# An FFT convolution on one NeuronCore: a second stage of 32 interleaved blocks with a shuffle, or of 16 wide blocks on rows paired +n and -n

## The chip, the cores and the metric

The kernel runs on one core of a Trainium2 chip. The core has a matrix engine (TensorE, PE in the profile; its weight loads are listed as PEld), three engines for elementwise work (VectorE or DVE, ScalarE or ACT, GpSimd or POOL), and SyncE (SP), which here does nothing but issue DMAs. POOL issues DMAs too. Each engine takes its own instructions in order and waits on semaphores for the others. The metric is the device time of one execution in microseconds (us), and a comparison of two kernels goes by the medians of their runs.

## The reference

Two computations are chained: a gated attention with squared ReLU in place of a softmax, and a gate with a long circular convolution, done as a Fourier transform over the S = 3136 rows.

```python
# u, v: [8, 3136, 256]   z: [8, 3136, 64]
scores = (1.0 / S) * np.matmul(z, z.transpose(0, 2, 1))
attn = np.maximum(scores, 0.0) ** 2
x = u * np.matmul(attn, v)                      # attention's output
proj = x @ w_proj                               # [.., 768]
x1, x2, x3 = proj[..., :256], proj[..., 256:512], proj[..., 512:]
X2 = np.fft.rfft(x2, n=S, axis=1)
H = np.fft.rfft(filter_fft, n=S, axis=0)[None]
x2_conv = np.fft.irfft(X2 * H, n=S, axis=1)
return (x1 * x2_conv * x3) @ w_out
```

## The kernel before

**Rows and chunks.** A row n is split as n = n1 * 49 + n2 with n1 < 64 and n2 < 49. A tile of 128 rows holds two values of n2, 64 rows for each, so that a batch has 25 tiles (NT), the last one half full. The 25 tiles of a batch form seven chunks of 512, 384, 512, 384, 512, 384 and 448 query columns (`CHUNKS`). In the kernel before, tile t holds n2 = t and n2 = 25 + t.

**Attention.** For each chunk, pairs of tiles are scored (`score_mm`, L1299: two 64-row matmuls), ACT takes the ReLU (L1474), ACT or DVE squares (L1481, L1483), and the squares are multiplied with v into two PSUM banks (`weigh`, L1329). A part of the squares is transposed by DMA on SP's queue and used again for another chunk (`mirror`, L1414). `xe` (L1527, DVE) multiplies the sum with u^T.

**Projection.** `add_proj` makes the gate x1 * x3 (`ev3`, L865, DVE) and x2 (L893), and `dft1` (L724) applies the first stage of the transform, a [128, 128] table T1 that does both 64-point transforms of a tile. Its result goes to DRAM (D1).

**Second stage.** `add_spectrum` reads D1 back in eight pieces `qq` of four blocks each. A block is 49 complex numbers as 98 interleaved rows and 256 channels. For each piece: one DMA load (L754), four matmuls of 98x98 tables S2 by 256 columns in two groups (L943), two evictions to `xh`, then on DVE a `stream_shuffle` (L964) that swaps real and imaginary rows, two products with H (L967) and a difference (L970), four matmuls with TZ (L1001), two evictions, and a DMA store to D2 (L1031). The last batch has no shuffle: it forms two products (`mul2`, L974) and runs eight matmuls a piece (L1008) against TZ and a copy of TZ with rows swapped. Its pieces also use buffers of other pools, and its loads may run four ahead (`l_p` has four buffers).

**End.** `add_end` loads D2 by groups of four tiles (L765), applies T4 (L1063), multiplies by the gate (L1070, DVE, one instruction for each stretch of a chunk that the group covers), multiplies by w_out (L1101), evicts and stores (L1128).

**Start.** POOL first issues the loads of v and u for batch 0, and behind them its iota instructions (L447 on), from which DVE and ACT build the tables T1, then S2 in eight steps of 392 columns (L588 to L596, L643, L644) and a ninth for block 0. Once, under batch 0, the filter goes through the same stages and gives H (L792 to L794, L807, L356, L360).

**Order.** The order of the instructions of every engine is written when the kernel is built, by the class `Plan`: it simulates the five engines with the costs that each task names, a task becomes ready from the planned ends of the ones before it, and SP's transfers get a planned landing from `moves`, `late`, `DMA_GO` and `DMA_DONE`. PE takes from three kinds of queue: scores (S), the weighing (W) and the fillers (FA the projection, FB the second stage and the end, FZ the ends of batch 6 that are held back for the last batch). At run time the order is fixed, so whatever is late holds up all that is behind it on its engine.

## Time and profile before

| | |
|---|---|
| median of 3 runs | 1052.53 us |
| lowest and highest | 1052.33, 1054.18 us |
| span of the profiled execution (first to last instruction) | 1056.2 us |
| busy in the span | PE 1002.7, ACT 930.4, DVE 841.3, POOL 175.9 us |
| DMA | 325263 packets, 168.35 MB, 159 GB/s; SP's queue 59.8% and POOL's queue 20.9% of 16 engines |

The profiled execution has a span of 1056.2 us, which is 3.7 us above the median of the runs and 2.0 us above the slowest of them. Durations in the profile are from that one execution. Its page lists for each group of instructions the line, the engine, the operation, the tiles and shapes, the count, the busy time, the mean duration of one, and the idle time of the engine just before the group with what ended it. The timeline lists the instructions in order: start, length, engine, line. A row with "x4" merges four of them. SPq is SP issuing a DMA. The table by stretches lists for each engine the busy time in a stretch with the number of instructions behind it, then the granted clock, the DMA share and GB/s. A matmul's listed duration contains the time until its result is out, in which the next one already runs.

### The profile page before, as it was taken

Reading aid. Unit: us, or ns where it says so; the run is one execution under the profiler, and the core shown is the slowest. Engines: PE = TensorE matmul, PEld = TensorE weight load, DVE = VectorE, ACT = ScalarE, POOL = GpSimd, SP = SyncE. Lnnn points to the kernel's source line nnn. Section 1 sums busy time; section 2 is a strip of 40 time slices with the busy share of each in tenths; the row PEclk is TensorE's granted clock in tenths of the full one; section 3 lists DMA queues with packets and bytes.
Section 4 is the critical chain, followed back from the end, with each engine's and each line's share of the span. In section 5 each row is a group of like instructions: output and inputs, shape, how many; then the busy total and the mean of one; then the engine's idle time right before and its main releaser. Section 6 shows DMA issues by size and latency. Waiting matters only on the chain.

```text
span 1056.2 us, 18580 instructions
## 1 busy us (share of the span) xinstructions
PE 1002.7 (95%) x6335; PEld 511.0 (48%) x6335; DVE 841.3 (80%) x1449; ACT 930.4 (88%) x1326; POOL 175.9 (17%) x355
## 2 busy tenths in 40 slices
PE   5899999999999999999999999999999999999984
PEld 2443444445444544454455444545455444554573
DVE  7976678986889778997789958888788887889673
ACT  7897799997999989997999989989998899889772
POOL 3031301221022120212021310121112120001000
PEclk9999999999999999999999999999999999999997
DMA  9489836889698787898799767997789968786486
GB/s 180 74 165 162 153 76 148 151 158 178 163 162 164 136 177 168 189 154 126 169 204 180 135 139 147 181 202 130 148 163 198 179 129 158 158 187 123 115 247 202
DMA packets 325263, 168.35 MB, mean 159 GB/s; under 512 B 232766, under 2 KB 295230, under 8 KB 325168
## 3 DMA queue, kind: packets, MB, share of 16 engines
q1 hardware_dynamic: 301824, 136.19, 59.8%
q0 software_dynamic: 23344, 30.97, 20.9%
q8 instruction: 50, 0.82, 0.3%
q14 instruction: 45, 0.37, 0.1%
HBM read 90.26 MB, written 53.05 MB: 136 GB/s over the span
## 4 chain that ended last, share of the span: by engine, by line
PE 72%; DVE 9%; DMA 8%; ACT 6%; issue 3%; SPq 1%; POOL 1%; DVEq 0%; ACTq 0%; POOLq 0%
PE ps_o_t L1329 37%; PE ps_s_t L1299 11%; DMA M_t<-A_t 5%; PE ps_m_t L893 3%; PE ps_m_t L859 3%; PE ps_m_t L1101 3%; PE ps_m_t L847 3%; ACT R_t L1474 3%; PE ps_m_t L724 2%; PE ps_m_t L1001 2%; PE ps_m_t L1063 2%; DVE xT_t L1527 2%; PE ps_m_t L943 2%; DVE xh L967 1%; DMA specf<-s_t 1%
## 5 line engine op out<-in xcount | busy, mean ns | idle before, releaser
L1474 ACT ACTIVATE R_t<-ps_s_t 128x1024 f32<-128x1024 f32 (+2 forms) x552 | 488.5, 922 | 34.5 <-PE ps_s_t L1299 26.2
L1329 PE MATMUL ps_o_t<-A_t,v_t 128*128 128x512 bf16 (+2 forms) x2064 | 475.1, 355 | 1.9 <-DVE A_t L1483 1.5
L1329 PEld LDWEIGHTS <-v_t 128*128 128x128 bf16 x2688 | 253.9, 98 | 215.9 <-issue 42.2
L1483 DVE TENSOR_TENSOR A_t<-R_t 128x1024 bf16<-128x1024 f32 (+3 forms) x276 | 298.9, 1090 | 32.2 <-ACT R_t L1474 21.3
L1481 ACT ACTIVATE A_t<-R_t 128x768 bf16<-128x768 f32 (+3 forms) x276 | 257.1, 949 | 10.4 <-DMA M_t<-A_t 7.3
L1299 PE MATMUL ps_s_t<-zT_t 64*128 64x512 bf16 (+2 forms) x1088 | 155.1, 357 | 4.5 <-ACT R_t L1474 4.3
L392 POOL COPY tick<-xT_t 1x1 bf16<-1x1 bf16 x54 | 26.6, 492 | 778.7 <-DVE xT_t L1527 778.7
L1527 DVE SCALAR_TENSOR_TENSOR xT_t<-ps_o_t,uT_t 128x384 bf16<-128x384 f32 (+2 forms) x128 | 69.9, 557 | 26.2 <-PE ps_o_t L1329 16.6
L354 ACT ACTIVATE x_t<-ps_m_t 128x512 bf16<-128x512 f32 (+3 forms) x139 | 73.7, 549 | 17.0 <-PE ps_m_t L847 14.0
L1070 DVE TENSOR_TENSOR yT_t<-ps_m_t,gate_t 128x128 bf16<-128x128 f32 (+4 forms) x166 | 63.1, 425 | 27.3 <-PE ps_m_t L1063 27.1
L1299 PEld LDWEIGHTS <-zT_t 64*128 64x128 bf16 x1088 | 33.1, 94 | 103.2 <-issue 102.3
L865 DVE TENSOR_TENSOR gate_t<-ps_m_t,x_t 128x512 bf16<-128x512 f32 (+2 forms) x110 | 65.6, 618 | 20.0 <-PE ps_m_t L859 16.8
L1329 PE MATMUL ps_o_t<-M_t,v_t 128*128 128x384 bf16 (+2 forms) x336 | 77.8, 345 | 3.3 <-DMA M_t<-A_t 3.3
L358 DVE CAST x_t<-ps_m_t 128x512 bf16<-128x512 f32 (+3 forms) x90 | 54.6, 621 | 22.4 <-PE ps_m_t L893 13.4
L967 DVE TENSOR_TENSOR xh<-xh,H 98x1024 bf16<-98x1024 bf16 x112 | 72.3, 684 | 0.0
L387 POOL DMA_DIRECT2D un_t<-in_u_dram x112 | 59.7, 551 | 6.9 <-issue 4.6
L847 PE MATMUL ps_m_t<-xT_t,wp 128*128 128x512 bf16 (+2 forms) x224 | 57.5, 353 | 2.5 <-DVE xT_t L1527 1.4
L893 PE MATMUL ps_m_t<-wp,xT_t 128*128 128x256 bf16 x392 | 58.2, 273 | 1.5 <-DVE gate_t L865 1.4
L859 PE MATMUL ps_m_t<-xT_t,wp 128*128 128x512 bf16 (+2 forms) x220 | 55.5, 355 | 0.4 <-DVE gate_t L865 0.2
L354 ACT ACTIVATE xh<-ps_m_t 98x512 bf16<-98x512 f32 x86 | 50.5, 614 | 3.7 <-PE ps_m_t L943 2.5
L1329 PE MATMUL ps_o_t<-M2e_t,v_t 128*128 128x512 bf16 (+1 forms) x192 | 51.7, 370 | 1.1 <-DVE xT_t L1527 1.1
L358 DVE CAST s_t<-ps_m_t 128x512 bf16<-128x512 f32 (+2 forms) x66 | 41.4, 630 | 12.6 <-PE ps_m_t L724 10.9
(168 smaller groups left out, 1026.2 us busy)
## 6 DMA issues: line engine op xcount, KB each, us to landing
out_dram<-ost_t SPq DMA_DIRECT2D x82, 256.0 KB
spec_in_t<-spec SPq DMA_DIRECT2D x64, 196.0 KB
spec<-gs_t SPq DMA_DIRECT2D x60, 196.0 KB
spec<-s_t SPq DMA_DIRECT2D x80, 128.0 KB
v_t<-in_v_dram POOLq DMA_DIRECT2D x80, 128.0 KB, 4.1
spec_in_t<-spec SPq DMA_DIRECT2D x39, 256.0 KB
un_t<-in_u_dram POOLq DMA_DIRECT2D x56, 128.0 KB, 4.9
un_t<-in_u_dram POOLq DMA_DIRECT2D x56, 96.0 KB, 4.5
```

Source lines behind the costliest of these rows:

```text
L354: nc.scalar.activation(out_, in_, AF.Copy)
L358: nc.vector.tensor_copy(out_, in_)
L847: nc.tensor.matmul(box["p"][:, :cw], wp16[:, k, ds(nb * P, P)], xt["t"][:, k, :cw], start=(k == 0), stop=(k == 1),)
L859: nc.tensor.matmul(box["p3"][:, :cw], wp16[:, k, ds((4 + nb) * P, P)], xt["t"][:, k, :cw], start=(k == 0), stop=(k == 1),)
L893: nc.tensor.matmul(box["p"][:rows, ds(k_ * D, D)], xt["t"][:, k, ds((i + k_) * P, rows)], wp16[:, k, ds(D, D)], start=(k == 0), stop=(k == 1),
L967: nc.vector.tensor_tensor(xb["z"][:KR, i], xb["z"][:KR, i], H[:KR, qq, i], ALU.mult)
L1299: nc.tensor.matmul(ps[:m, i, :cw], zt[h, ds(t * P, m)], zt[h, ds(C0[c], cw)], start=True, stop=True)
L1329: nc.tensor.matmul(o, row(v16[b], t)[:, ds(dh * P, P)], x, start=(k == 0 and i == 0), stop=(last and i == len(pair) - 1),)
L1474: nc.scalar.activation(box["R"][:rows, 0:n, :cw], live[un][:rows, 0:n, :cw], AF.Relu)
L1481: nc.scalar.activation(a, r, AF.Square)
L1483: nc.vector.tensor_tensor(a, r, r, ALU.mult)
L1527: nc.vector.scalar_tensor_tensor(x, f, inv_s2, ut, ALU.mult, ALU.mult)
```

## The change

The tiles are filled in another order and the second stage is cut in another way. Nothing in what is computed changes.

- **Pairing.** n2 is counted around its middle, so that a tile holds rows n2 and the rows that mirror them (+n and -n). The loads of z, u and v are cut by chunk (`runs`), since the first half of a tile runs backwards through a chunk. `xe` and `ev3` become two instructions each, one for each half, and the first one writes its tiles in reverse order. `add_end` works by chunk: the gate is one instruction for each half of the channels, and T4's matmul writes two stretches of 64 columns.
- **First stage.** T1 gives 32 real and 32 imaginary lines of the pair's sums and differences, so that real and imaginary parts stand side by side in the columns.
- **Second stage.** 16 blocks j (NJ) of 2 x 50 rows. A block is one matmul of a 128x128 real table by 512 columns, 256 real and 256 imaginary (`forward`, `inverse`); block 0 takes four of 256. The product with H has two multiplications with H repeated over the two halves, and two instructions of half the size for the difference and the sum; no shuffle. D1 is read in four loads of four blocks, each of two DMAs of 50 partitions with 4 KB each, and D2 is written likewise. The last batch takes the same way with eight loads and stores of two blocks, two DMAs each; the swapped table and `mul2` are gone.
- **Tables.** S2 and TZ have 19 tables of 128x128 in place of 32 of 98x98. S2 needs two steps of 392 columns and one of 50. H takes 15 matmuls of 512 columns and 4 of 256, and 16 evictions, in place of 64 and 32; its expanded tables (L792 to L794) are gone.
- **Buffers.** `l_p` has two buffers of twice the size, and the loads of the end get their own pool `c_p` with two; `gs_p` doubles. Two memsets on POOL clear the unused rows.

The diff, cut to its core:

```diff
-NQ = 32
-KR = 2 * N2
+NJ = 16
+KB = 50
...
-    gs_p = Pool("gs", 2, [P, 4, D], BF16)
-    l_p = Pool("spec_in", 4, [P, 4, D], BF16)
+    gs_p = Pool("gs", 2, [P, 8, D], BF16)
+    l_p = Ring("spec_in", 2, [P, 8, D], BF16)
+    c_p = Pool("conv_in", 2, [P, 4, D], BF16)
...
+    def runs(lo, hi):
+        got = []
+        for c in range(NC):
+            a, b = max(lo, T0[c]), min(hi, T0[c + 1])
+            if a < b:
+                got.append((0, a, b, NT - T0[c + 1] + a - T0[c]))
+        if lo < min(hi, NT - 1):
+            got.append((1, lo, min(hi, NT - 1), NT + lo))
+        return got
+
+    def halves(c):
+        n = len(tiles[c])
+        return (0, n), (1, n if CHUNKS[c] % P == 0 else n - 1)
+
+    def by_half(x, h, n):
+        return x.rearrange("p (t i) -> p t i", i=P)[:, 0:n, ds(h * N1, N1)]
...
+        for j, lo, hi, n2 in runs(t0, t1):
+            for c in range(home[lo], home[hi - 1] + 1):
+                a, b = max(lo, T0[c]), min(hi, T0[c + 1])
+                nc.gpsimd.dma_start(
+                    out=t[ds(j * N1, N1), ds(v_at(a), (b - a) * D)],
+                    in_=r[:, n2 + a - lo : n2 + b - lo, :].rearrange("p t d -> p (t d)"),
+                )
...
-    load_rows(v16[0], v[0], 0, 8)
+    load_rows(v16[0], v[0], 0, 7)
     u_nat = {}
     cast_u(0, 0)
-    load_rows(v16[0], v[0], 8, NT)
+    load_rows(v16[0], v[0], 7, NT)
+    k1v, k2v, k0v = kcol[:, 0:N1], kcol[:, N1 : N1 + 8 * N2], kcol[:, 456:512]
+    nc.gpsimd.iota(k1v, pattern=[[N2, N1 // 2], [0, 2]], base=0, channel_multiplier=0)
...
-    for q0 in range(0, NQ, 4):
+    for j0 in (0, 8):
...
+            for r in range(2):
+                nc.sync.dma_start(
+                    out=box["t"][ds(r * N1, KB), 0 : 2 * nj, :], in_=by_block(src, r)[:, ds(2 * j0, 2 * nj), :]
+                )
+
+        t = on("SP", go, 0.9, [pads, *deps, *((d, ISSUED) for d in loads[-1:])], [l_p.slots], moves=0.6 * nj, late=late)
...
+    def two_tables(ps, w, x, order):
+        for c, pair in enumerate(order):
+            for k, i in enumerate(pair):
+                nc.tensor.matmul(
+                    ps[:, ds(c * D, D)], w[:, i, :], x[:, ds(k * D, D)], start=(k == 0), stop=(k == 1)
+                )
+
+    def forward(ps, x, j):
+        if j:
+            nc.tensor.matmul(ps[:, :], S2[:, 3 + j, :], x, start=True, stop=True)
+        else:
+            two_tables(ps, S2, x, ((3, 0), (1, 2)))
...
-                    nc.vector.tensor_tensor(
-                        gates[b, c, nb][:, :cw], box["p3"][:, :cw], box["x"][:, :cw], ALU.mult
-                    )
+                    for h, w in halves(c):
+                        g, p, x = (by_half(y, h, w) for y in (gates[b, c, nb], box["p3"], box["x"]))
+                        nc.vector.tensor_tensor(g[:, ::-1] if h == 0 else g, p, x, ALU.mult)
...
+            def mul(i, g=g, xb=xb):
+                x = xb["x"][:].rearrange("p i (j c) d -> p i j c d", c=2)
+                h = H[:, ds(2 * g, 2), i].unsqueeze(2).to_broadcast([P, 2, 2, D])
+                nc.vector.tensor_tensor(x[:, 1 - i], x[:, 0], h, ALU.mult)
+
+            def sums(xb=xb):
+                x = xb["x"][:].rearrange("p i (j c) d -> p i c j d", c=2)
+                nc.vector.tensor_tensor(x[:, 1, 0], x[:, 1, 0], x[:, 0, 1], ALU.subtract)
+                nc.vector.tensor_tensor(x[:, 1, 1], x[:, 1, 1], x[:, 0, 0], ALU.add)
...
+                    for k in range(nt):
+                        lo, hi = (nt - 1 - k) * P, k * P + N1
+                        x = cb["t"][:, k, ds(dh * P, P)]
+                        o = box["p"][:, 0:512]
+                        if hi >= w:
+                            nc.tensor.matmul(o[:, ds(lo, N1)], x, T4[:, 0:N1], start=True, stop=True)
+                            continue
+                        o = bass.AP(o.tensor, o.offset + min(lo, hi), [o.ap[0], [abs(hi - lo), 2], [1, N1]])
+                        nc.tensor.matmul(o, x, T4[:, ds(N1 if lo > hi else 0, P)], start=True, stop=True)
```

## The prediction

> **What bounds the kernel now.** I read the page first, then the table by stretches, the groups by form, and the timeline of start and tail. The stretches from 160 to 1000 us, summed, show an idle PE for 840 - 826.4 = 13.6 us in all; PE sets the pace there, and what DVE and ACT save can give back little of it. The columns are length, then busy time (instructions) of PE, PEld, DVE, ACT, POOL, then clock, DMA share, GB/s.
>
> ```profile
> 0.00:40.00 40.00, 26.42 (x137) 10.51 (x138) 32.40 (x88) 31.99 (x48) 10.56 (x29) 1.00 0.66 121
> 80.00:120.00 40.00, 34.96 (x194) 15.61 (x192) 23.65 (x41) 29.88 (x38) 7.03 (x15) 0.96 1.04 164
> 640.00:680.00 40.00, 40.00 (x282) 20.62 (x280) 33.91 (x57) 38.03 (x53) 5.55 (x12) 1.00 0.89 174
> 1000.00:1040.00 40.00, 28.96 (x234) 22.95 (x233) 25.80 (x55) 24.20 (x47) 0.00 (x0) 0.85 0.81 242
> ```
>
> So the change must be priced in PE time in the middle, and in whatever is late at both ends. The timeline shows what a matmul costs in a row of them, and the start:
>
> ```profile
> 1014.59 0.27 PE L1008 MATMUL ps_o_t<-xh,TZ 98*98 98x256 bf16 x1
> 1014.70 0.27 PE L1008 MATMUL ps_o_t<-xh,zT_t 98*98 98x256 bf16 x1
> ...
> 21.02 2.76 PE L1329 MATMUL ps_o_t<-A_t,v_t 128*128 128x512 bf16 x12
> ...
> 1.51 1.34 POOL L399 DMA_DIRECT2D v_t<-in_v_dram  x2
> ...
> 6.17 0.36 POOL L447 IOTA yT_t<- 128x128 int32 x1
> 6.56 0.47 DVE L612 TENSOR_SCALAR spec_in_t<-yT_t,percol 128x64 f32<-128x64 int32 x2 [2.87 <-POOL yT_t L447]
> 8.18 0.31 ACT L596 ACTIVATE T<-spec_in_t 128x128 bf16<-128x128 f32 x1 [3.45 <-DVE spec_in_t L593]
> 8.39 0.58 ACT L354 ACTIVATE zT_t<-ps_m_t 128x512 bf16<-128x512 bf16 x1
> 9.11 1.04 PE L1299 MATMUL ps_s_t<-zT_t 64*128 64x512 bf16 x4
> ```
>
> A 256-column matmul lasts 0.27 us but the next starts after 0.11; twelve of 512 columns take 2.76, of which 0.38 is the last one's length, so (2.76 - 0.38) / 11 = 0.216 each. And the first scores hang on POOL's iota: POOL's loads, then the iota, DVE, ACT's sine, the copy of z behind it in ACT's queue, the scores. The groups that the change removes or replaces:
>
> ```profile
> L967 DVE TENSOR_TENSOR xh<-xh,H 98x1024 bf16<-98x1024 bf16 x112 | 72.3, 684 | 0.0
> L943 PE MATMUL ps_m_t<-spec_in_t,S 98*98 98x256 bf16 x244 | 43.9, 275 | 0.3
> L964 DVE STREAM_SHUFFLE xh<-xh 128x512 f32<-128x512 f32 x56 | 39.8, 729 | 0.4 <-issue 0.4
> L970 DVE TENSOR_TENSOR xh<-xh 98x1024 bf16<-98x1024 bf16 x56 | 38.7, 692 | 1.7
> L724 PE MATMUL ps_m_t<-x_t,T 128*128 128x512 bf16 x79 | 29.7, 382 | 0.4 <-ACT x_t L354 0.2
> L1195 DVE COPY zd_t<-zn_t 128x1024 bf16<-128x1024 bf16 x21 | 8.8, 419 | 0.2 <-DMA zn_t<-in_z_dram 0.2
> ```
>
> **The change, part by part.**
>
> *PE, per spectrum.* Forward and inverse are 64 matmuls x 0.109 = 7.0 us now and 2 x (15 x 0.216 + 4 x 0.109) = 7.35 after: +0.35, over seven batches +2.5 us. The busy column agrees: single 512-column matmuls show 29.7 / 79 = 0.376 against 2 x 43.9 / 244 = 0.36 for the pair that one replaces. Half as many instructions buy PE nothing.
>
> *DVE, per spectrum.* Gone: 8 shuffles x 0.729 = 5.8 and 8 differences x 0.692 = 5.5. New: 16 half-size instructions. In the rows a DVE instruction has about 0.15 us that doesn't shrink (512 columns from PSUM 0.687, 256 0.416), so each is (0.692 + 0.15) / 2 = 0.42, in all 6.7. The two products stay at 0.684 if H, repeated, is read at full rate; L1195, which repeats its input the same way, takes 0.419 for 1024. Halving `xe` and `ev3` adds 0.15 us for each extra instruction, 12 + 14 = 26 of them: +3.9. The end's gates go from 24 pieces to 14 a batch: -1.5. Sum -2.2 us a batch on an engine that isn't the bound, hidden by PE; at most 13.6 us of PE's idle time could answer to it. `xe` frees PSUM for PE, so some of its 0.15 shows. ACT's evictions stay 16 + 16. DMAs on SP per batch are the same number within two (loads 8 and 8, stores 8 and 8, outputs 13 and 14). POOL issues about 4 more loads of z and 1 of v per batch, 0.55 us each, on an engine busy 17%; the same hides its memsets and the filter's loads, now partly in pieces of 1 KB. The end's loads get two buffers where they shared four, behind W work as before. Late loads (below) can add. Together for the seven spectra: +1 (-6 to +8), nearest to PE's row.
>
> *Start.* Batch 0's v goes out in 4 + 11 POOL DMAs instead of 2 + 4. Nine more at 0.55 (mean of L399) to 0.67 (1.34 / 2) put the iota 5 to 6 us later, and T1 takes four small DVE instructions where two stood, less two memsets: first scores +5.5. DVE, ACT and PE all wait in order behind it, so nothing covers it. z's ten SP DMAs for six come 3 us later at most and are landed by then. Against this, six of eight table steps go from DVE and ACT: 2 x 0.382 + 0.365 + 0.365 + 0.562 + 2 x 0.15 = 2.36 us on DVE and 0.53 on ACT each, 17 us in all. Between 10 and 40 us DVE is busy 27.9 and ACT 28.1 of 30 and PE 24.7, so there they are the bound. With the work shared out, half of it, 8.7 us, is the most it can give, and PE's own idle time of 5.3 is nearer. I take 4. Net +1.5 (-3 to +5).
>
> *H and the tables.* Matmuls for H 64 x 0.109 = 7.0 become 3.7, the transposes lose 0.4; the 16 evictions and the expanded tables (8 x 0.92 on DVE) that go had little to hold up, since DVE and ACT are 59% and 75% busy from 80 to 120 us, where PE's waits are for DMAs that stay. -4 (-8 to -1).
>
> *Tail.* The last batch's second stage runs from the first load at 1007 us to the last store at 1030.3. Its DVE chain goes from 2 x 0.685 to 2 x 0.684 + 2 x 0.42 = 2.2 us a piece, +6.7 over eight; DVE is busy 11.8 of 12 us from 1012 to 1024. PE falls from 96 x 0.109 to 7.35, at a clock of 0.72 in the last 6 us. The loads: four could be out before, two now, each of two DMAs.
>
> ```profile
> 1007.50 1.82 SPq L754 DMA_DIRECT2D spec_in_t<-spec  x3
> 1013.28 3.15 SPq L754 DMA_DIRECT2D spec_in_t<-spec  x4
> 1019.43 0.38 PE L943 MATMUL ps_m_t<-spec_in_t,S 98*98 98x256 bf16 x2
> ```
>
> Already here the fifth piece starts at 1019.43, 6 us after its load was issued. Two at a time, at 3.4 us a landing (the chain's row for the first) plus about 1.5 to issue and compute, make four rounds of 5: last forward at about 1011 + 15 = 1026, then 4.4 us of DVE, inverse, eviction and store: 1033 to 1036 against 1030.3, less what PE saves. The end behind it is 25 tiles as before. +4 (0 to +7).
>
> **Sum.** 1.5 - 4 + 1 + 4 = +2.5. The profiled span of 1056.2 is 3.7 above the median of the runs, 1052.5; I put the differences on the median: 1055.0 us. A change within 0.2%, 2.1 us, I count as none: about what a measurement of this kernel can tell.
>
> **Rivals.**
>
> *Faster: the first 160 us belong to DVE and ACT.* In the start they do, and the work taken from them there is 17 + 7.4 + 16 x 0.63 = 34 us. If they set the pace up to H as well, half, 17 us, comes off, in place of the 8 I count for recovery and H together: 1055.0 - 9 = 1046. It decides once more than 10.5 us are recovered. PE's idle time speaks for it (20.8 us in 160, 8.3 in the first 10), DVE and ACT at 59% and 75% before H against.
>
> *Slower: the blocks land late in all batches.* A load is 392 KB instead of 196, through 50 partitions at a time, and the plan gives it 1.2 + 2.4 + 0.8 + 1.0 = 5.4 us after its issue. If the landing grows with the bytes from 3.4 to 6.8, each is 1.4 late; 28 of them, if PE stood for each, 39 us. PE stood only 2.1 us for such loads at L943 before, the W work ahead of them covers most, and I take a quarter: 1065. It decides when landings pass the planned ones by more than the next PE group. The Trainium skill, "DMA: Bandwidth & Descriptors", section "Why a DMA increments its semaphore by 16 and not by 1", says that a DMA uses the largest number of engines up to 16 that divides the slowest dimension: 14 for 98 rows, but 10 for 50. By that rule each engine carries 40 KB instead of 14, and this rival gains; the views, means over 16 engines, don't show it.
>
> *Slower: no full rate for H repeated.* At the rate of the f32 squares (1.219 for 1024) 16 products cost +0.535 and 16 half instructions +0.27 each, 12.9 us a batch; DVE would then be as busy as ACT, and I put 15 us: 1070. L1195 speaks against it.
>
> **How the numbers follow.** The forecast, parts that nearly cancel, 0.50: its range is 1047 to 1063, of which slower 0.28, within 0.2% 0.17, faster 0.05. Faster rival 0.30 (0.28 faster, 0.02 same), late blocks 0.15, no full rate 0.05. In all: faster 0.33, same 0.19, slower 0.48. The range to the other cases, leaving out a tenth on either side: 1043 to 1066.
>
> **What would show it.** Start: first L1299-type scores near 14.6 us instead of 9.11, with DVE waiting for the iota. Recovery: the first `xe` no later than 37 us (35.4 now). PE: 512-column matmuls of the second stage 0.216 apart, and an idle sum from 160 to 1000 us near 13.6; well above, the late blocks are right. DVE: products near 0.68, sums near 0.42. Tail: last D2 store 3 to 6 us further behind the last weighing. I am wrong if the start isn't delayed, or if PE's waits in the middle change by more than 6 us.

## The result and the profile after

The changed kernel takes 1069.2 us (median of four runs, 1065.5 to 1071.4) where the one before, run beside it, takes 1053.4 (1052.3 to 1056.1). The ratio is 1.0146, with a 95% interval of 1.0116 to 1.0177: slower, as was held likeliest in sign, but by 16 us and not by 2.5, and 3 us past the end of the range.

The profiled execution has a span of 1069.5 us against 1056.2 before, 13.3 more. Split at two points that both traces have, the first `xe` of batch 1 and the first of the very last chunk, it is 2.1 us ahead of the kernel before at the first point, loses 10.9 between the two, and 4.5 in the tail behind the second: -2.1 + 10.9 + 4.5 = 13.3. The medians lie 15.9 apart, so the two profiled executions show a little less than the whole. The forecast had -2.5, +1 and +4. The miss is the middle.

The table by stretches of the changed kernel, with the columns as before (length, busy time and instructions of PE, PEld, DVE, ACT and POOL, then the clock, DMA share and GB/s):

```profile
0.00:40.00 40.00, 17.01 (x91) 6.84 (x92) 22.64 (x59) 21.30 (x34) 17.79 (x37) 1.00 0.68 117
80.00:120.00 40.00, 39.72 (x235) 18.00 (x232) 28.59 (x48) 36.00 (x48) 15.36 (x32) 1.00 1.12 175
640.00:680.00 40.00, 39.78 (x259) 19.42 (x257) 33.50 (x57) 39.66 (x54) 4.38 (x10) 1.00 0.76 169
1000.00:1040.00 40.00, 29.21 (x158) 13.56 (x155) 32.13 (x61) 23.89 (x43) 0.00 (x0) 0.76 0.45 133
```

The first 40 us lost 9.4 us of PE (26.42 before). From 80 to 120 PE is full where it idled 5 us before: the lighter H and tables pay the start back there. The stretch from 640 on looks as before; the middle's loss sits in a few places and has to be looked for. In the last row PE's clock is 0.76 against 0.85. Summed over the 21 stretches of 40 us from 160 to 1000, PE idles 16.5 us against 13.6, which is 2.9 more and far less than the 10.9 lost. Where the rest hides is the first thing to learn here. A matmul at half clock counts as busy, and so does work that the changed kernel does between the two points and the kernel before did elsewhere; both are measured in the account of the prediction below.

The groups that replace those shown of the kernel before:

```profile
L969 DVE TENSOR_TENSOR xh<-xh,H 128x1024 bf16<-128x1024 bf16 x120 | 81.4, 683 | 5.6 <-ACT xh L357 4.7
L793 PE MATMUL ps_m_t<-spec_in,S 128*128 128x512 bf16 x123 | 45.8, 384 | 3.7 <-ACT R_t L1456 1.7 <-DVE gs_t L361 1.0 <-ACT H L359 0.4
L973 DVE TENSOR_TENSOR xh<-xh 128x512 bf16<-128x512 bf16 x60 | 25.3, 422 | 1.7
L974 DVE TENSOR_TENSOR xh<-xh 128x512 bf16<-128x512 bf16 x60 | 25.0, 416 | 0.0
```

The products with H repeated keep their 0.683 us and the sums take 0.42: both as priced, and the rival of a lost rate is out. Nor do the forward matmuls wait for their loads. So the middle lost its time neither to the rate of DVE nor, directly, to late blocks.

The start, in the timeline of the changed kernel:

```profile
7.75 0.52 POOL L416 DMA_DIRECT2D v_t<-in_v_dram  x1 [0.92 <-DMA v_t<-in_v_dram]
...
10.30 0.52 POOL L416 DMA_DIRECT2D v_t<-in_v_dram  x1 [0.66 <-DMA un_t<-in_u_dram]
...
13.38 0.32 POOL L457 IOTA yT_t<- 128x64 int32 x1
13.73 0.85 DVE L630 TENSOR_SCALAR gs_t<-yT_t,percol 128x32 f32<-128x32 int32 x4 [10.24 <-POOL yT_t L457]
16.71 0.31 ACT L616 ACTIVATE T<-gs_t 128x128 bf16<-128x128 f32 x1 [12.42 <-DVE gs_t L612]
18.96 1.03 PE L1281 MATMUL ps_s_t<-zT_t 64*128 64x512 bf16 x4 [0.58 <-ACT zT_t L357]
```

The iota comes at 13.38 instead of 6.17, and the first scores at 18.96 instead of 9.11: 9.85 us, where 5.5 were forecast. From its eleventh DMA on, POOL waits before four of seven for an earlier one to land (0.92, 0.66, 0.59 and 0.23, in all 2.4 us), which the count of issues left out. Behind the iota, the second conversion of z (L361, 0.95 us at 16.59) now stands on DVE behind the steps of the pattern, where ACT had made the first two from 4.01 on in the kernel before, so z's own path to the scores waits for the pattern too.

The largest step of the middle is 6.2 us beside the kernel before, between the fifth and sixth chunk of batch 1. In the timeline of the changed kernel there:

```profile
240.31 0.96 DVE L1465 TENSOR_TENSOR A_t<-R_t 128x768 bf16<-128x768 f32 x1 [3.02 <-DMA M2e_t<-A_t]
...
241.36 0.92 ACT L1456 ACTIVATE R_t<-ps_s_t 128x896 f32<-128x896 f32 x1 [3.27 <-DVE A_t L1465]
241.92 0.38 PE L731 MATMUL ps_m_t<-x_t,T 128*128 128x512 bf16 x1 [2.99 <-DVE x_t L361]
```

DVE's next square stands 3.02 us for a transposing DMA that still reads the buffer it needs; ACT, the copies behind the square, and PE stand with it. What SP's queue did just before, in the kernel before and in the changed one:

```profile
228.19 1.23 SPq L1202 DMA_TRANSPOSE zT_t<-zd_t  x1
...
230.58 1.21 SPq L1158 DMA_TRANSPOSE uT_t<-un_t  x1
231.84 2.33 SPq L1414 DMA_TRANSPOSE M2e_t<-A_t  x1
```

```profile
228.82 0.82 SPq L1016 DMA_DIRECT2D spec<-gs_t  x2
229.74 3.07 SPq L1188 DMA_TRANSPOSE zT_t<-zd_t  x1
232.91 1.23 SPq L1144 DMA_TRANSPOSE uT_t<-un_t  x1
234.19 2.58 SPq L1396 DMA_TRANSPOSE M2e_t<-A_t  x2
```

In the changed kernel the transpose of z, right behind two stores of second-stage blocks, holds SP for 3.07 us instead of 1.23, and the mirrored tile's transposes leave some 2.3 us later. And the clock after the wait, in stretches of one microsecond of the same trace:

```profile
239.00:240.00 1.00, 0.00 (x0) 0.00 (x0) 0.00 (x0) 0.00 (x0) 0.00 (x0) 1.00 1.24 157
...
242.00:243.00 1.00, 1.00 (x5) 0.51 (x5) 1.00 (x2) 0.88 (x2) 0.00 (x0) 0.72 0.42 127
243.00:244.00 1.00, 1.00 (x5) 0.43 (x3) 0.92 (x2) 0.22 (x1) 0.00 (x0) 0.50 0.14 44
244.00:245.00 1.00, 1.00 (x6) 0.20 (x6) 0.51 (x1) 0.38 (x1) 0.00 (x0) 0.50 0.30 90
245.00:246.00 1.00, 1.00 (x9) 0.27 (x8) 0.00 (x0) 0.45 (x1) 0.00 (x0) 0.57 0.00 0
```

After its 2.99 us of rest PE gets half clock for 3.4 us: 0.28 + 0.50 + 0.50 + 0.43 = 1.7 us more, in which it shows as busy. The wait and the clock explain 4.7 of the step's 6.2 us.

### The profile page after: what moved, and what is told of

It reads as the page before. It is cut to its first block, busy times and chain, and to the rows that moved or that the text cites. A ratio compares the mean times of both kernels' runs of the same rounds, so it can differ in the third digit from the quotient of the medians.

```text
span 1069.5 us, 17972 instructions
## 1 busy us (share of the span) xinstructions
PE 998.4 (93%) x6029; PEld 468.0 (44%) x6029; DVE 827.9 (77%) x1492; ACT 914.6 (86%) x1282; POOL 189.9 (18%) x405
## 4 chain that ended last, share of the span: by engine, by line
PE 51%; DVE 7%; DMA 3%; ACT 3%; issue 2%; SPq 1%; DVEq 0%; ACTq 0%
PE ps_o_t L1311 26%; PE ps_s_t L1281 7%; PE ps_m_t L1086 3%; PE ps_m_t L897 2%; PE ps_m_t L866 2%; PE ps_m_t L854 2%; DVE A_t L1465 2%; PE ps_m_t L1055 2%; DVE xh L969 2%; DMA M2e_t<-A_t 2%; PE ps_m_t L799 1%; PE ps_m_t L731 1%; DVE xT_t L1505 1%; PE ps_m_t L793 1%; ACT R_t L1456 1%
## 5 line engine op out<-in xcount | busy, mean ns | idle before, releaser
L1465 DVE TENSOR_TENSOR A_t<-R_t 128x768 bf16<-128x768 f32 (+4 forms) x286 | 305.1, 1073 | 55.7 <-ACT R_t L1456 37.4
L1463 ACT ACTIVATE A_t<-R_t 128x1024 bf16<-128x1024 f32 (+4 forms) x266 | 252.8, 956 | 11.3 <-DMA M2e_t<-A_t 3.3
L406 POOL COPY tick<-xT_t 1x1 bf16<-1x1 bf16 x54 | 10.8, 200 | 760.4 <-DVE xT_t L1505 760.4
L874 DVE TENSOR_TENSOR gate_t<-ps_m_t,x_t 128x256 bf16<-128x256 f32 (+1 forms) x222 | 72.7, 382 | 39.4 <-PE ps_m_t L866 32.0
L1505 DVE SCALAR_TENSOR_TENSOR xT_t<-ps_o_t,uT_t 128x256 bf16<-128x256 f32 (+1 forms) x224 | 76.2, 381 | 26.2 <-PE ps_o_t L1311 14.9
L969 DVE TENSOR_TENSOR xh<-xh,H 128x1024 bf16<-128x1024 bf16 x120 | 81.4, 683 | 5.6 <-ACT xh L357 4.7
L357 ACT ACTIVATE x_t<-ps_m_t 128x512 bf16<-128x512 f32 (+3 forms) x116 | 62.3, 562 | 20.3 <-PE ps_m_t L854 10.9
L1058 DVE TENSOR_TENSOR yT_t<-ps_m_t,gate_t 128x512 bf16<-128x512 f32 (+2 forms) x99 | 59.6, 620 | 25.2 <-PE ps_m_t L1055 21.7
L361 DVE CAST x_t<-ps_m_t 128x512 bf16<-128x512 f32 (+3 forms) x105 | 62.4, 612 | 12.6 <-PE ps_m_t L897 8.4
L416 POOL DMA_DIRECT2D v_t<-in_v_dram x112 | 59.5, 555 | 6.4 <-issue 2.1
L854 PE MATMUL ps_m_t<-xT_t,wp 128*128 128x512 bf16 (+2 forms) x222 | 56.5, 352 | 2.9 <-DVE xT_t L1505 2.5
L357 ACT ACTIVATE xh<-ps_m_t 128x512 bf16<-128x512 f32 (+1 forms) x91 | 55.0, 626 | 1.2 <-PE ps_m_t L793 0.8
L1086 PE MATMUL ps_m_t<-wo,yT_t 128*128 128x256 bf16 (+1 forms) x346 | 54.4, 277 | 0.6 <-DVE yT_t L1058 0.3
```

What stands on the lines that cost most here:

```text
L357: nc.scalar.activation(out_, in_, AF.Copy)
L854: nc.tensor.matmul(box["p"][:, :cw], wp16[:, k, ds(nb * P, P)], xt["t"][:, k, :cw], start=(k == 0), stop=(k == 1),)
L969: nc.vector.tensor_tensor(x[:, 1 - i], x[:, 0], h, ALU.mult)
L1086: nc.tensor.matmul(box["p"][:rows, ds(i * D, D)], yb["y"][:, k, ds((i0 + i) * P, rows)], wo16[:, k, :], start=(k == 0), stop=(k == 1),)
L1463: nc.scalar.activation(a, r, AF.Square)
L1465: nc.vector.tensor_tensor(a, r, r, ALU.mult)
```

## The experiments

Times are set against the kernel before run on the same chip (medians 1053 to 1055). The landmarks come from one profiled execution of each kernel, read from its timeline in us: the first `xe` of the kernel, of batch 1 and of the last chunk, and the tail from there to the end of the span. The middle is how much more time lies between the second and third landmark than in the kernel before. A profiled execution can stand some 7 us from its kernel's median (three mends 6.3 below, four mends 6.9 above), and that of the run with four loads stands 9.6 above. The two variants of the kernel before have tails of 56.4 and 56.5 with nothing altered there, and two runs alike in the middle, the four mends with early and with later pads, differ by 3.1 in it. So landmarks say where and ratios say how much, and 2 us in the tail or 3 to 4 in the middle of a single profile decide nothing.

| kernel | ratio to before (95%) | first | batch 1 | last | middle | tail |
|---|---|---|---|---|---|---|
| before | 1 | 35.4 | 164.4 | 997.6 | 0 | 58.6 |
| changed | 1.0146 (1.0116 to 1.0177) | 45.0 | 162.3 | 1006.4 | +10.9 | 63.1 |
| patterns first | 1.0063 (1.0030 to 1.0095) | 35.3 | 156.1 | 996.9 | +7.6 | 61.9 |
| ten squares | 1.0087 (1.0058 to 1.0117) | 45.4 | 161.0 | 997.8 | +3.6 | 62.9 |
| four loads | 1.0207 (1.0158 to 1.0256) | 43.0 | 164.4 | 1026.1 | +28.5 | 56.7 |
| no sums at the end | 1.0102 (1.0070 to 1.0135) | 46.6 | 162.2 | 1005.7 | +10.3 | 57.8 |
| z in eights | 1.0191 (1.0161 to 1.0221) | 45.5 | 164.7 | 1012.7 | +14.8 | 62.7 |
| before, z in sevens | 0.9979 (0.9954 to 1.0004) | 35.5 | 161.8 | 995.6 | +0.6 | 56.4 |
| before, nine squares | 1.0019 (0.9999 to 1.0039) | 35.5 | 163.6 | 1001.1 | +4.3 | 56.5 |
| three mends | 0.9962 (0.9942 to 0.9982) | 36.2 | 150.5 | 985.5 | +1.8 | 56.2 |
| blocks cut 48 + 2 | 1.0143 (1.0103 to 1.0182) | 44.6 | 165.2 | 1004.6 | +6.2 | 64.1 |
| stores cut 48 + 2 | 1.0100 (1.0061 to 1.0139) | 45.7 | 163.6 | 1003.4 | +6.6 | 62.2 |
| four mends | 0.9958 (0.9935 to 0.9980) | 35.9 | 154.6 | 992.6 | +4.8 | 60.1 |
| four mends, pads later | 0.9958 (0.9937 to 0.9979) | 36.2 | 149.7 | 984.6 | +1.7 | 60.7 |
| squares and stores | 1.0093 (1.0057 to 1.0129) | 45.9 | 160.2 | 1002.7 | +9.3 | 61.7 |
| z in two DMAs | 1.0165 (1.0127 to 1.0203) | 45.2 | 167.1 | 1010.6 | +10.3 | 62.0 |
| best | 0.9934 (0.9908 to 0.9960) | 36.0 | 153.3 | 991.8 | +5.3 | 56.2 |

### The start: index patterns ahead of v's loads

```diff
+    k1v, k2v, k0v = kcol[:, 0:N1], kcol[:, N1 : N1 + 8 * N2], kcol[:, 456:512]
+    nc.gpsimd.iota(k1v, pattern=[[N2, N1 // 2], [0, 2]], base=0, channel_multiplier=0)
...
     load_rows(v16[0], v[0], 0, 7)
     u_nat = {}
     cast_u(0, 0)
     load_rows(v16[0], v[0], 7, NT)
-    k1v, k2v, k0v = kcol[:, 0:N1], kcol[:, N1 : N1 + 8 * N2], kcol[:, 456:512]
-    nc.gpsimd.iota(k1v, pattern=[[N2, N1 // 2], [0, 2]], base=0, channel_multiplier=0)
...
```

> The changed kernel, with POOL's index patterns (the iotas and the one-column memset between them) issued ahead of all of batch 0's v loads, nothing else altered. Both theories: the first iota ends before 3 us instead of at 13.7, and the first scores come at 9 to 11 us instead of 18.96. Theory 'the start's delay stands': PE sets the pace behind the start, so nothing pays the 9.85 us back, and the end comes 6 to 10 us earlier, 1059 to 1063 beside 1069.2. Theory 'absorbed': batch 1 was already 2.1 us ahead of the kernel before in spite of the late start, so the first 160 us are held by something else than the first scores; the first xe of batch 1 stays within 2 us of 162.2 and the time within 2 us of 1069.2.

The timeline of this kernel:

```profile
1.36 0.29 POOL L453 IOTA yT_t<- 128x64 int32 x1
...
3.56 0.80 DVE L630 TENSOR_SCALAR gs_t<-yT_t,percol 128x32 f32<-128x32 int32 x4
5.58 0.31 ACT L616 ACTIVATE T<-gs_t 128x128 bf16<-128x128 f32 x1 [1.38 <-DVE gs_t L612]
...
7.23 1.03 PE L1281 MATMUL ps_s_t<-zT_t 64*128 64x512 bf16 x4 [0.58 <-ACT zT_t L357]
```

DVE no longer waits for the pattern, and the scores start at 7.23, before those of the kernel before and earlier than expected. The ratio falls from 1.0146 to 1.0063, 0.83% of 1053 or 8.7 us: the start's delay stands to the end. Of its 9.7 us at the first `xe`, 6.2 are still there at batch 1, and 9.5 at the last chunk. "Absorbed" was wrong, and my reading of batch 1 with it. This run is 8.3 us ahead of the kernel before there, so the lighter tables and H are worth some 8, and in the changed kernel they cover the late start. The delay costs what they gain. The middle's step of 6 us in batch 1 is unmoved.

### The middle: ten buffers for the squares

```diff
-    A_p = Pool("A", 8, [P, 1024], BF16)
+    A_p = Pool("A", 10, [P, 1024], BF16)
```

> The changed kernel with 10 buffers for the squares (A) instead of 8. Between the fifth chunk of batch 1 and the last of batch 2 it loses some 10 us against the kernel before, and there DVE waited 3.02 us and ACT 3.11 us for the transposing DMAs that read an A buffer. Theory 'buffers': two more let the squares go on while those DMAs land; the two waits go, and 5 to 10 us with them: 1059 to 1064. Theory 'the transposes themselves are late': the W matmuls that read the mirrored tile wait instead, and the time stays within 2 us of 1069.2.

The chain of waits by pair (total, times, longest), of the changed kernel and of this one:

```profile
DVE A_t L1465 <- DMA M2e_t<-A_t: 6.9, 4, 3.0
...
ACT A_t L1463 <- DMA M2e_t<-A_t: 3.3, 2, 3.1
```

```profile
DVE A_t L1465 <- DMA M2e_t<-A_t: 1.7, 1, 1.7
```

The two waits go (the 1.7 us that are left stand at 108 us, in the start), the step of 6.2 us in batch 1 goes entirely, and 0.59% (6 us) of the time comes back. The transpose of z still holds SP, now for 3.57 us at 234.1, but the squares go on meanwhile. "Buffers" holds, though something of the other theory is seen too: PE's own waits for mirrored tiles rise from 0.2 to 4.1 us. Is this a shortage that the kernel before had too? There, beside a larger H, nine were tried:

```diff
-    A_p = Pool("A", 8, [P, 1024], BF16)
+    A_p = Pool("A", 9, [P, 1024], BF16)
```

> The kernel before with 9 buffers for the squares instead of 8 (10 do not fit beside its H of 32 KB a partition). Theory 'the change made the buffers short': the kernel before has no such wait to lose, its PE idles 13.6 us from 160 to 1000 in all, and its time stays within 2 us. Theory 'both kernels are short of them': it gains 2 to 6 us, and what the second run showed is worth as much without the change.

1.0019: no gain. But the premise, that the kernel before has no such wait, does not stand. Its waits by pair have this one:

```profile
ACT A_t L1481 <- DMA M_t<-A_t: 7.3, 4, 3.8
```

DVE adds one of 1.8 us. The longest, 3.8 us, stands at 87 us, under the filter; the three behind 160 us are 1.3, 1.8 and 2.0 us long, and no half clock follows them. The changed kernel has five there, with 3.0 and 3.1 the longest. Nine buffers leave 7.2 of the 9.1 us, all of it in the start, and PE's own waits for mirrored tiles grow from 3.3 to 11.3 us. So the squares' buffers were short at times before the change too, and with it the waits in the middle became longer. That the kernel before would gain nothing from two more buffers, as the changed kernel had, is not shown. What makes the transposes late?

### Not the fourth piece of z, nor its third DMA

```diff
-            t0, t1 = 7 * i, min(7 * i + 7, NT)
+            t0, t1 = 8 * i, min(8 * i + 8, NT)
```

> The changed kernel with z of the following batch loaded and transposed in pieces of 8, 8, 8 and 1 tiles, as in the kernel before, instead of 7, 7, 7 and 4; two of the pieces then take 4 DMAs, one 3 and the last one 1. Theory 'the fourth piece': in the changed kernel a transpose of 4 tiles instead of 1 stands in SP's queue in the fifth chunk, ahead of the mirrored tiles' transposes, and makes them late where DVE and ACT waited 3.02 and 3.11 us for the A buffer; without it the steps of 6.2 us from the fifth to the sixth chunk of batch 1 and 4.4 us in batch 2 (beside the kernel before) go, and the time falls by 4 to 9 us. Theory 'not z': both steps stay, and the time is within 2 us of the changed kernel's 1.0146 of before.

The reverse, in the kernel before:

```diff
-            t0, t1 = 8 * i, min(8 * i + 8, NT)
+            t0, t1 = 7 * i, min(7 * i + 7, NT)
```

> The kernel before with z of the following batch in pieces of 7, 7, 7 and 4 tiles: this part of the change alone, two DMAs a piece as it has. Theory 'the fourth piece': it loses 4 to 9 us, at the fifth chunks of batches 1 and 2. Theory 'not z': within 2 us of before.

Both refute it: pieces of eight make the changed kernel no faster (1.0191, some 5 us above 1.0146, with intervals that overlap; the step in batch 1 is 4.3 us), and pieces of seven cost the kernel before nothing (0.9979). That kernel's transposes of seven tiles take 1.2 us of SP as the others do, all but two, so the length of the piece is not what holds the queue. Fewer DMAs for it on POOL:

```diff
-                    cast_rows(box["n"], z[n], t0, t1, True)
+                    x = rows_n1(z[n])
+                    if t1 == NT:
+                        nc.gpsimd.dma_start(out=box["n"][N1:P, t1 - 1 - t0, :], in_=x[:, NT - 1, :])
+                    for j in range(2):
+                        hi = min(t1, NT - j)
+                        nc.gpsimd.dma_start(
+                            out=box["n"][ds(j * N1, N1), 0 : hi - t0, :], in_=x[:, NT * j + t0 : NT * j + hi, :]
+                        )
```

> The changed kernel with each piece of the next batch's z loaded by two DMAs from consecutive rows, as in the kernel before, instead of three (what is left out: z's rows of batches 1 to 7 come in another order). Theory 'POOL's extra DMAs share in the middle loss': 3 to 6 of the 10.9 us go. Theory 'z is no part of it': within 3 us of 10.9, which is what two profiles of kernels alike from batch 1 on (the runs with and without later memsets) differed by.

The middle's loss is 10.3 and the ratio 1.0165: the extra loads of z are no part of it.

### The blocks of 50 partitions

```diff
             for r in range(2):
-                nc.sync.dma_start(
-                    out=box["t"][ds(r * N1, KB), 0 : 2 * nj, :], in_=by_block(src, r)[:, ds(2 * j0, 2 * nj), :]
-                )
+                for lo, n in ((0, 48), (48, KB - 48)):
+                    nc.sync.dma_start(
+                        out=box["t"][ds(r * N1 + lo, n), 0 : 2 * nj, :],
+                        in_=by_block(src, r)[lo : lo + n, ds(2 * j0, 2 * nj), :],
+                    )
...
                     for r in range(2):
-                        nc.sync.dma_start(
-                            out=by_block(D2[b % 2], r)[:, ds(2 * j0, 2 * per), :], in_=gx["g"][ds(r * N1, KB), 0 : 2 * per, :]
-                        )
+                        for lo, n in ((0, 48), (48, KB - 48)):
+                            nc.sync.dma_start(
+                                out=by_block(D2[b % 2], r)[lo : lo + n, ds(2 * j0, 2 * per), :],
+                                in_=gx["g"][ds(r * N1 + lo, n), 0 : 2 * per, :],
+                            )
```

> The changed kernel with every load and store of the second stage's 50-partition blocks cut in two DMAs, of 48 and 2 partitions. In the changed kernel SP spent 2.9 to 3.6 us on 8 of 28 transposes of z, and 1.2 on each of the kernel before's but one; of 17 transposes that it issued within 3 us behind a 50-partition store (200 KB, always two), 9 took over 2 us. Theory 'the 50-partition blocks hold the queue': the long transposes go, the mirrored tiles land in time, DVE's and ACT's waits of 3.02 and 3.11 us for the A buffer go, and from the fifth chunk of batch 1 to the last of batch 2 the kernel loses 0 to 4 us beside the one before, not 10.7; time 1059 to 1065. Theory 'the bytes hold the queue, however cut': the long transposes stay, and SP's extra issues (16 a batch at 0.4 us) change nothing or cost: 1068 to 1073. The Trainium skill, 'DMA: Bandwidth & Descriptors', section 'Why a DMA increments its semaphore by 16 and not by 1', has 10 engines for 50 partitions and 16 for 48, so by that rule the first theory holds.

And the second half of the diff alone:

> The changed kernel with only the stores of the blocks cut in 48 and 2 partitions, the loads as they are. Theory 'the stores hold the queue': as the run with both cut, within 2 us. Theory 'loads and stores alike': half of that gain, 2 to 4 us. Theory 'the bytes': no gain.

The transposes of z as a group, with min, median and max ns, in the changed kernel, with all cut, and with only the stores cut:

```profile
L1188 SPq DMA_TRANSPOSE zT_t<-zd_t x28: 1221/1257/3552, 92.5 to 866.7; - x28
```

```profile
L1192 SPq DMA_TRANSPOSE zT_t<-zd_t x28: 1194/1250/1919, 92.7 to 863.1; - x28
```

```profile
L1190 SPq DMA_TRANSPOSE zT_t<-zd_t x28: 1188/1252/2929, 92.9 to 863.6; - x28
```

The same bytes in the same place no longer hold SP: of the six transposes of z over 2.8 us (the expectation's eight took in two of nearly 2) none is left with all cut, one with the stores cut. The step in batch 1 falls from 6.2 us to 1.6 and 2.3. So it isn't the bytes alone. That the partitions decide it is argued: the cut also makes two DMAs of one, and a cut in 25 + 25, which would tell the two apart, wasn't run. The rule of the Trainium skill, "DMA: Bandwidth & Descriptors", section "Why a DMA increments its semaphore by 16 and not by 1", of 10 engines for 50 partitions and 16 for 48, fits; the views show no single engine, so the count itself isn't seen here. Nor are such stores the only thing that holds SP: the kernel before has transposes of mirrored tiles of up to 3.47 us that stand behind other DMAs.

The times are less clear than the traces. The stores alone take back 0.46% (5 us), with an interval that overlaps the changed kernel's. With the loads cut too the ratio is 1.0143, which is the time of the other theory, "the bytes", and not within 2 us of the stores alone. The middle gains as much there (6.2 and 6.6), but the profile is 1.6 us later than with the stores alone at batch 1, where one stretch of half clock stands at 143 us, and its tail is 1.9 us longer. And a late mirrored tile still holds a buffer and stops PE in both: 1.95 us at 261 us with all cut, 2.88 us at 383 with the stores cut.

Are the buffers and the cut stores two mends of one loss? Both, with the stores of the last batch left whole:

> The changed kernel with 10 buffers for the squares and, in all batches but the last, the stores cut in 48 and 2 partitions. From the first xe of batch 1 to the last xe the changed kernel lost 10.9 us beside the one before; 10 buffers alone left 3.6 of it, the cut stores alone 6.6. Theory 'one loss': the stores make the mirrored tiles late and the squares' buffers stand for them, so either mend takes back the same microseconds; together 2 to 5 us are left and the time is that of the 10 buffers alone (1.0087 of before) within 2 us. Theory 'two losses': they add, and 0 us or less are left; 1.004 to 1.006.

1.0093 beside 1.0087: one loss, by the time. But the middle of its profile still shows 9.3 us, not 2 to 5. This profiled execution lies 3.9 us above its kernel's median and that of ten squares 2.1 below, so the 5.7 us between the two middles are of the executions and not of the kernels. The timeline shows where 6 of them went, at the end of batch 2, and the stretches behind it the clock:

```profile
383.09 1.60 PE L1313 MATMUL ps_o_t<-M_t,v_t 128*128 128x448 bf16 x4 [2.97 <-DMA M_t<-A_t]
```

```profile
382.00:383.00 1.00, 0.00 (x0) 0.00 (x0) 0.00 (x0) 0.97 (x2) 0.00 (x0) 1.00 1.00 216
383.00:384.00 1.00, 0.91 (x3) 0.41 (x4) 0.00 (x0) 0.76 (x1) 0.00 (x0) 0.60 0.12 34
384.00:385.00 1.00, 1.00 (x5) 0.52 (x4) 0.00 (x0) 0.00 (x0) 0.00 (x0) 0.50 0.00 0
385.00:386.00 1.00, 1.00 (x7) 0.67 (x6) 0.42 (x1) 0.00 (x0) 0.00 (x0) 0.50 0.00 0
386.00:387.00 1.00, 1.00 (x6) 0.53 (x5) 0.84 (x2) 0.00 (x0) 0.00 (x0) 0.69 0.00 0
```

Here the weighing itself waits for a mirrored tile, for which no square's buffer helps: 2.97 us, then 1.7 to the clock. A wait of 3 us took nearly 5, in both places. In the 21 stretches of the middle the kernel before has no stretch under full clock, the changed one has one (0.96), and this one has two; but the two variants of the kernel before have one each, at 745 and 748 us.

### The tail: four loads, or no sums

Four whole buffers, and POOL's clearing of them moved, in one run that is read at both ends:

```diff
-    l_p = Ring("spec_in", 2, [P, 8, D], BF16)
+    l_p = Ring("spec_in", 4, [P, 8, D], BF16)
...
-    pads = after(on("POOL", pad_zero, 4.0, lat=0.3), 14.0)
+    pads = after(on("POOL", pad_zero, 4.0, lat=0.3), 40.0)
```

> The changed kernel with four buffers for the spectrum's loads instead of two, and the memsets that clear them (eight now, four before) moved from 14 us to 40 us of the plan; two edits, read at two ends. Tail, theory 'loads two deep': with four in flight the last D2 store is 32 to 33 us behind the last weighing instead of 36.2, and the time falls by 3 to 4 us there. Tail, theory 'DVE chain': eight pieces of 2.1 us set it, and it stays at 35 to 36. Start, theory 'DVE is slowed by the memsets': L664, 1.19 us beside a memset and 0.48 later, takes 0.5, and the first xe comes 1.5 to 3 us before 45.0; otherwise it stays within 1 us of 45.0. Together: 1063 to 1066 if both first theories hold, 1069 if neither.

The last batch without its sums:

```diff
-            z_ = on("DVE", sums, 2 * c_dve2(2 * D), [w_], prio=ZP)
+            z_ = w_ if final else on("DVE", sums, 2 * c_dve2(2 * D), [w_], prio=ZP)
```

> The changed kernel without the two sums of each piece in the last batch's second stage (its output for that batch lacks the cross terms): 0.84 of DVE's 2.1 us a piece. Theory 'DVE chain': the eight pieces run at DVE's pace, and the last D2 store comes 4 to 6.7 us closer to the last weighing than 36.2. Theory 'loads two deep': each round of two loads saves one piece's sums at most and waits for the next load, 0.8 to 2 us in all.

The stretches of 8 us from 16 us behind the last weighing on: the changed kernel (two of them), then four loads, then no sums:

```profile
1022.90:1030.90 8.00, 4.86 (x11) 1.02 (x9) 7.03 (x13) 4.78 (x9) 0.00 (x0) 0.50 0.44 139
1030.90:1038.90 8.00, 5.11 (x13) 1.57 (x14) 7.12 (x15) 4.44 (x9) 0.00 (x0) 0.50 0.79 238
```

```profile
1042.60:1050.60 8.00, 5.18 (x23) 1.83 (x22) 7.86 (x17) 8.00 (x18) 0.00 (x0) 0.95 0.80 241
```

```profile
1022.30:1030.30 8.00, 4.13 (x14) 1.23 (x13) 5.83 (x9) 5.55 (x12) 0.00 (x0) 0.86 0.61 183
```

And the rounds of the changed kernel in its timeline:

```profile
1022.35 2.31 SPq L764 DMA_DIRECT2D spec_in<-spec  x4
...
1026.03 0.61 PE L799 MATMUL ps_o_t<-xh,TZ 128*128 128x512 bf16 x1 [2.05 <-DVE xh L974]
...
1028.54 2.18 SPq L764 DMA_DIRECT2D spec_in<-spec  x4
...
1032.09 0.61 PE L799 MATMUL ps_m_t<-xh,TZ 128*128 128x512 bf16 x1 [2.05 <-DVE xh L974]
```

Either edit brings the last D2 store from 36.0 us behind the last weighing (32.2 in the kernel before) to 30: 29.9 with four loads, 30.1 without sums. The expectations set the two causes against each other, and both came true, the one of the loads by more than it had (32 to 33). The rounds show why. In each, two pieces are loaded, DVE works on them while PE stands 2.05 us for it, and the next loads go out only when PE has taken the buffers: 6.2 us from loads to loads. Load and DVE chain stand in one line, and the rests keep PE at half clock (0.50 for some 20 us in the second stage, against 3 before), where its matmuls take 0.61 and not 0.38 us. Taking out either shortens the round, and the clock comes back, to 0.95 and 0.86 in the 8 us shown.

Four loads everywhere cost 28.5 us in the middle of the profile (by the ratios the whole kernel loses some 6 against the changed one), in steps of about 7 such as those at the ends of batches 3 and 4, and from 480 to 520 us with the clock at 0.91 and 0.94. That the second stage then runs ahead and leaves none of its work to fill these places is argued from the plan, not shown. The pads are read below.

### Together

The patterns first, ten squares, and in the last batch alone four half buffers cut from the two:

```diff
+    class HalfRing:
+
+        def __init__(self, ring):
+            self.tiles = [t[:, 4 * i : 4 * i + 4, :] for i in range(2) for t in ring.tiles]
+            self.slots, self.n = Slots(len(self.tiles)), 0
...
+    lh_p = HalfRing(l_p)
...
-                ldb[0] = load_spec(D1[b % 2], 2 * g, per, puts, LATE_LOAD * (not final))
+                ldb[0] = load_spec(D1[b % 2], 2 * g, per, puts, LATE_LOAD * (not final), lh_p if final else l_p)
```

> The changed kernel with three edits: the index patterns ahead of v's loads, 10 buffers for the squares, and in the last batch's second stage four half-size load buffers cut from the same two tiles, so that four loads are in flight there and two elsewhere. If the three add up as their own profiles have them (8.8 at the start, 7 in the middle by the last xe less what the start gave, 6 in the tail) from 1.0146 of before: last xe some 8 us ahead of the kernel before, last D2 store 30 us behind the last weighing, time 0.990 to 0.998 of before, the first that is faster. If the start's gain is lost again in the middle, as in the first run from batch 1 to batch 2: 0.998 to 1.004.

0.9962: faster than the kernel before. The last D2 store is 30.0 us behind the last weighing and the tail 56.2, which is that of the two variants of the kernel before. With all loads and stores cut as well, and then with the pads later:

> The three mends together (index patterns ahead of v's loads, 10 buffers for the squares, four half-size load buffers at the end; 0.9962 of before) and the loads and stores cut in 48 and 2 partitions. Theory 'the extra buffers already cover the late transposes': within 0.2% of 0.9962. Theory 'late transposes still cost': in that run some 5 us were lost from batch 1 to the end beside the kernel before, mostly at the last chunks of batches 2 to 4; 3 to 5 us come back, 0.991 to 0.994. Against: in the tail 32 more DMAs on SP at 0.4 us each, 1 to 3 us if SP sets the pace there.

> The same with POOL's four memsets of the load buffers moved from 14 us to 40 us of the plan. Theory 'DVE is slowed by the memsets': as in the run with four loads, where the first xe came 2.0 us earlier, it comes 1 to 3 us earlier here, and as PE sets the pace behind it the time falls by as much. Otherwise both stay within 1 us.

The cut adds nothing to the time (0.9958): 16 more loads and 16 more stores take 3.9 us in the tail, 60.1 instead of 56.2. That the cut gives as much back in the middle follows from the medians; the profiles don't show it (4.8 and 1.7 against 1.8). The later pads change neither the first `xe` (36.2 and 35.9) nor the time, so the memsets were no cause of the slow start. In the run with four loads the first `xe` did come 2.0 us earlier, but there DVE's steps stood behind a late pattern and beside the memsets. The two profiles are 4.9 us apart at batch 1, but not for the pads: the three mends with early pads stand at 150.5 too. Two stretches of 40 us at 0.96 clock, from 80 and 120 on, stand in the first and none in the second.

So the cut is left to the stores of the first seven batches, and the loads stay whole:

```diff
-                        for lo, n in ((0, 48), (48, KB - 48)):
+                        for lo, n in ((0, KB),) if final else ((0, 48), (48, KB - 48)):
```

> The three mends (index patterns ahead of v's loads, 10 buffers for the squares, four half-size load buffers at the end) with the stores cut in 48 and 2 partitions in all batches but the last. The run with all loads and stores cut ended 59.5 us behind the last weighing where the three mends alone ended 55.7: the cut cost 3.8 us in the tail, and the medians were alike, so it gave some 4 us in the middle. Theory 'that is the whole of it': 3 to 4 us below the three mends, 0.992 to 0.993 of before. Theory 'the gain in the middle came from the loads': within 0.2% of 0.9962.

1046.0 us beside 1053.0: 0.9934 (0.9908 to 0.9960), the fastest of all; by the ratios some 22 us under the change as it was made. Against the three mends it is 0.28% better, as the first theory had it, but the two intervals overlap, so this last step isn't shown.

## Why the prediction was right and wrong

- **PE per spectrum** held: 512-column matmuls start 0.22 us apart (1017.06 and 1017.28 in the tail at full clock), so half the instructions bought nothing.
- **DVE per spectrum** held: products 0.683, sums 0.42. PE's one rest over 0.9 us in the middle for a sum, 1.45 us at 852 us, comes behind a wait of DVE's for a buffer of the squares.
- **Start**: mis-sized. The first scores came 9.85 us late, not 5.5. The step "nine more at 0.55 to 0.67" counted the issues and left out POOL's waits for earlier DMAs to land, 2.4 us from 7.75 on, and the steps behind the iota, priced as unchanged, took 5.58 us where 2.94 had been. The first `xe` was to come by 37 and came at 45.0.
- **Recovery and H**: 4 + 4 = 8 priced. The run with the patterns first stands 8.3 ahead at batch 1. The sizes held, but the recovery came only after the first 40 us. Start and H together were to be -2.5 and were -2.1: the start 4 us worse, and the recovery better by as much, most of it from 80 us on, where PE is now full. That the two misses cancel is luck.
- **Seven steady spectra, +1 (-6 to +8)**: this step failed; 10.9. The profiles divide it. Between the two landmarks PE is busy 821.3 of 833.2 us before and 828.1 of 844.2 after: 4.2 more of idle PE, 1.7 of half clock, and 5.0 more of work at full clock. The work is the same in every profile of the changed kernel that holds all matmuls, mends or not, 825.9 to 826.7. Of the 5.0, 2.5 were priced as PE's own cost. Counted in columns that the matmuls stream, 7,168 of the 15,616 more are the spectra's and 8,448 those of the ends of 11 tiles of batch 6: 322 of the 400 output matmuls stand ahead of the last chunk's `xe` after (L1086), 300 before (L1101). So about half of the 5.0 is work that the kernel before does in its tail, and no new cost. What failed is the price of the waits. It took them to fall a little (+1 where PE's row gave +2.5), and waits with the clock behind them cost 5.9 more, 4.7 of it in the one place in batch 1. It priced each engine's work and the loads, and left out what the new shape of the *stores* does to whatever SP issues next.
- **The path**, as far as it is followed: two stores of 50 partitions, a transpose of z that holds SP 3 us, a mirrored tile late, a square's buffer held, 3 us of rest on all three engines, 1.7 us of half clock. Ten buffers break it by trace and by time; the cut stores break it by trace, and by time not beyond the noise. The rival "the blocks land late in all batches" named the 50 partitions, but looked for PE waiting at loads (of 400 KB, not 392), of which L793 shows none. A sign stood on the page of the kernel before: 7.3 us of ACT's idle time before its squares ended with the transposes of mirrored tiles, and the prediction doesn't use it. The rival of a lost rate has the nearest time, 1070, and its mechanism is refuted: a near number shows nothing.
- **Tail, +4 (0 to +7)**: came out at 4.5, partly by luck. From its first load to its last D2 store the second stage takes 29.9 us where it took 23.3, since the rounds take 6.2 us, not 5, with a clock that I had not lowered for the matmuls. Against this, its first load goes out 6.1 us behind the last weighing and not 8.9; no run shows why.
- **What would make it wrong** was PE's waits changing by more than 6 us in the middle. Idle PE rose by only 2.9 from 160 to 1000 us, and the time by 10.9: the sign itself was too weak, since half clock and work from elsewhere hide in the busy column.

## What to carry to other kernels

Moving a tile's edge from 98 to 50 partitions left the price of the instructions nearly alone and changed which queue was clear for the next DMA: look at what is issued behind such a transfer, and try it cut (48 + 2 here). Give the buffers that a transpose reads enough depth to outlast its landing. Add to a wait of 2 to 3 us on PE the half clock that can follow it, which the busy column doesn't show. When two profiles are split at a landmark, count the matmuls on either side before a difference is called a loss. And do not count a gain in the start twice: it had covered a loss that could be undone by moving six lines.

## What the hardware showed

- A rest of 2.99 us on PE was followed by 3.4 us at 0.50 clock (1.7 us lost), and one of 2.97 likewise; at 368 us a rest of 2.1 us left the clock at 1.00. The length of the rest alone doesn't decide: half clock followed rests of 1.95 us (all blocks cut, 261 us) and 2.01 us (ten squares, 380 us) too. The Trainium skill, "TensorE: Matmul & The Clock Gate", section "What's actually happening", has the half clock after at least one idle window of some 3.4 us, in windows that run freely; the state and its length agree, while here 2 to 3 us of rest were enough.
- A transpose's issue can itself take 3 us on SP, where 1.2 is usual. In the changed kernel all six such transposes of z (2.9 to 3.6 us) stand right behind two 50-partition stores; with the blocks cut in 48 + 2 the longest takes 1.9 us.
- From its eleventh DMA on in the start of the changed kernel, POOL waited before four of seven issues for an earlier DMA to land, up to 0.92 us each.
